# Building C times B with fp32 matmuls against a diagonal of the step, and splitting the last table steps by unit, in a long-convolution and attention kernel

## The chip, the cores and the metric

The kernel runs on one core of one Trainium2 chip. The metric is the device time of one execution in microseconds (us). Five engines run their own queues of instructions and wait for each other by semaphores: PE (TensorE, matmuls), DVE (VectorE), ACT (ScalarE), POOL (GpSimd) and SP, which here only issues DMAs.

## The reference, cut to what matters

The program adds four factors to a 2048 x 512 input: a state-space convolution (A), a windowed attention (B), A again and B again, each on a layer norm of what stands so far. The two A factors have the same parameters, so their convolution kernel `K` is made once, in the first factor.

```python
dt = jnp.exp(log_dt)[:, None]                  # 512 x 1
A = A_re + 1j * A_im; Bc = B_re + 1j * B_im; Cc = C_re + 1j * C_im
logdA = dt * A; dB = dt * Bc
P = jnp.exp(logdA[:, :, None] * l[None, None, :])     # l = 0..2047
K = jnp.einsum("dn,dnl,dn->dl", Cc, P, dB).real
...                                            # y = FFT convolution of u with K, over 2 L points
x = x + _A_ref(_layernorm(x), ...)
x = x + _B_ref(_layernorm(x), wqkv, wo)
x = x + _A_ref(_layernorm(x), ...)
x = x + _B_ref(_layernorm(x), wqkv, wo)
```

## The kernel before

The powers of `exp(dt A)` are not computed one by one. `prepare` makes the first power `LAM` and squares it nine times (`lads`), `Multipliers` keeps the powers as bf16 multipliers (`MYA`, `MYB`, `MXA`, `MSA` and so on), and `Tables` builds from them, for each of eight units of 64 channels, a Y table, an X table and a B table (`Ytab`, `Xtab`, `Btab`). `contract` multiplies the tables on PE into kernel samples (`psk`), ACT or DVE copies them out (`kq`), `select` places them (`pk`, `KT`), and a two-stage FFT (`spectrum`: `ps_s`, `Z`, `zt`, `xp`) turns them into `sp_k`. The normed input goes the same way into `sp_u`. DVE multiplies the two (`pa`), PE goes back (`vp`, `ps_y`) and `X` is overwritten.

The seed of the tables is `cb`, the complex product of C, B and dt, turned so that the state index lies on the partitions. Before, DVE forms four products (`t1` to `t4`), one difference, one sum and two products with dt, into slots 2 and 3 of `quad`. PE transposes the four slots (`ptq`): slots 1 and 0 become `LAM`, slots 2 and 3 become `cb`.

In `table_ops` a step of the recurrence (`y0` to `y2`, `a`, `b`, `d`, `e` for Y; `x1` to `x4` for X) is a product pair (`T.times`) and, except for `x4`, a sum (`T.add`). `CHUNKS` groups the units: 0, 1, 6 and 7 alone, 2 with 3 and 4 with 5. For a pair of units all steps but `x3` are one instruction over both, and every unit of the pair waits for all of it.

The order of the work is not made by a scheduler at build time. Each layer has a `Plan`: operations are numbered as they are declared, some in several ways (`pl.either`, `moved`: the same copy by ACT or by DVE), and a line of numbers in `ORDERS` says which are issued and in which order. The engines then take their parts of it strictly in that order. `psA`, `psk` are PSUM pools of 3 and 2 buffers.

Other names that are used below: `xT`, the input turned by DMA transposes for the layer-norm sums (`gram`); `wqk`, `wv`, the attention's weights, from which a mean is taken out in the first factor, for each third either by PE and two ACT copies (`ps_wc`, 20 matmuls) or by PE, ACT and a DVE sum (`ps_wm`, 4 matmuls; `wm`); `identf`, an fp32 identity; `ps_down`, a small plain fp32 matmul in each attention factor, one per factor, so two in the program.

Of the kernel before, what the change touches and what calls it, by code (L numbers as in the profile page):

```python
# [11 lines left out]
ACT = mybir.ActivationFunctionType  # L12
ALU = mybir.AluOpType
AX = mybir.AxisListType
F32 = mybir.dt.float32
# [13 lines left out]
NM = 128  # L29
# [202 lines left out]
def load_params(nc, pp, prm):  # L232
# [14 lines left out]

GATES = (13,)
ORDERS = [
# [265 lines left out]
def table_ops(pl, nc, T, u, n, seeds, free, fixed, casts):  # L515
    e = T.elements

    def step(what, *after):
        out = []
        for v, m in ((u, 1), (u + 1, 1)) if n == 2 and what == "x3" else ((u, n),):  # L520
            us, key = e(m, what) / 1920 + 0.069, ("sc", v, what)
            a = pl.op("V", 2 * us + (0.06 if what in ("y1", "y2", "x1", "x2") else 0), lambda v=v, m=m: T.times(v, m, what), *after, casts[T.POWER[what]], take=[] if what == "x4" else key)
            if what != "x4":
                a = pl.op("V", us, lambda v=v, m=m: T.add(v, m, what), a, drop=key)
            out.append(a)
        return out
    y = moved(pl, nc, ("seed", u), 0.15 + 0.1 * n, 0.08 + 0.066 * n, lambda copy: T.seed(copy, u, n), seeds, free)
    x = moved(pl, nc, ("second", u), 0.15 + 0.1 * n, 0.08 + 0.066 * n, lambda copy: T.second(copy, u, n), casts[3], free)
    for what in ("y0", "y1", "y2", "a", "b", "d", "e"):
        y = step(what, y)  # L530
    x = step("x1", x, fixed)
    for what in ("x2", "x3", "x4"):
        x = step(what, x)
    return [y, x]


def vt(n):
# [3 lines left out]
def prepare(nc, pl, lp, pp, psA, psK, raw, identf, block, ones, M, cb, T, ln, X, D2, marks):  # L541
# [5 lines left out]
    def vec(us, fn, *after, **needs):  # L547
        return pl.op("V", us, fn, *after, **needs)

    def tt(out, a, b, op):  # L550
        return lambda: nc.vector.tensor_tensor(out, a, b, op)

    def got(name):
        return pl.outer(("raw", name))
# [3 lines left out]
    tb, e, sh, sn, t1, t2, t3, t4 = [tmp(x) for x in ("tb", "e_mag", "sh", "sn", "t1", "t2", "t3", "t4")]  # L558
    lads = lp.tile([128, 9, D], F32, name="lads", tag="sp_u")
    rnd = lads[:, 8].rearrange("n (t m) -> n t m", t=4)  # L560
    quad = pp.tile([128, 4, 4, NM], F32, name="quad", tag="quad")
    LAM = pp.tile([128, 2, D], F32, name="LAM0", tag="LAM")
    wide = dtw[:].unsqueeze(2).to_broadcast([128, 4, NM])
    dt_bc = dtf[:].unsqueeze(2).to_broadcast([128, 4, NM])
# [14 lines left out]
    qs = [vec(0.61, lambda: nc.vector.scalar_tensor_tensor(quad[:, :, 0, :], sh[:], 1.0, e[:], ALU.subtract, ALU.mult), o, oe),  # L579
          vec(0.61, tt(quad[:, :, 1, :], e[:], sn[:], ALU.mult), on, oe)]  # L580

    def stepped(q, src, after):

        def by_rows():
            for t in range(4):
                nc.scalar.activation(quad[:, t, q, :], src[:, t, :], ACT.Copy, scale=dtf[:, t:t + 1])
        return pl.either(("step", q), lambda: pl.op("A", 1.3, by_rows, after, of),
                         lambda: vec(0.61, tt(quad[:, :, q, :], src[:], dt_bc, ALU.mult), after, of))
    raws = [got(x) for x in ("C_re", "B_re", "C_im", "B_im")]
    a = vec(0.61, tt(t1[:], raw["C_re"][:], raw["B_re"][:], ALU.mult), raws[:2])  # L590
    b = vec(0.61, tt(t2[:], raw["C_im"][:], raw["B_im"][:], ALU.mult), raws[2:])
    a = vec(0.61, tt(t1[:], t1[:], t2[:], ALU.subtract), a, b)
    qs.append(stepped(2, t1, a))
    a = vec(0.61, tt(t3[:], raw["C_re"][:], raw["B_im"][:], ALU.mult), raws[0], raws[3])
    b = vec(0.61, tt(t4[:], raw["C_im"][:], raw["B_re"][:], ALU.mult), raws[1:3])
    a = vec(0.61, tt(t3[:], t3[:], t4[:], ALU.add), a, b)
    qs.append(stepped(3, t3, a))
    turns, modes = [], {}
    for q in (1, 0, 2, 3):
        def mm(q=q):  # L600
            pt = box["pt", q] = psK.tile([128, 4, NM], F32, name="ptq", tag="psk")
            for t in range(4):
                nc.tensor.transpose(pt[:, t, :], quad[:, t, q, :], identf[:])

        def evac(copy, q=q):
            pt = box.pop(("pt", q))
            if q < 2:
                out, src = LAM[:, q, :].rearrange("n (p t) -> n p t", t=4), pt[:].rearrange("n t p -> n p t")
                if q:
                    copy(out, src)  # L610
                elif copy == nc.scalar.copy:
                    nc.scalar.activation(out, src, ACT.Copy, scale=-1.0)
                else:
                    nc.vector.tensor_scalar(out, src, -1.0, None, ALU.mult)
            else:
                copy(cb[:, :, q - 2, :], pt[:].rearrange("n t p -> n p t"))
        key = ("psk", "ptq", q)
        turns.append(pl.op("P", 1.15, mm, qs[q], got("identf"), take=key))
# [141 lines left out]
def kernel_and_first_conv(nc, tc, C, prm, x2d, const, kt_dram, eps, Wt):  # L760
    with ExitStack() as es:
# [311 lines left out]
        for u in range(8):  # L1073
            for u0, n in CHUNKS:
                if u0 == u:
                    o = table_ops(pl, nc, T, u0, n, marks["seeds"], [Cd[x - 2] for x in range(u0, u0 + n) if x > 1], marks["fixed"], marks["casts"])
                    for x in range(u0, u0 + n):
                        Td[x] = o
            contract(u)
            dc = u // 2  # L1080
            if dc == 3:
# [921 lines left out]
```

## Time and profile before

| | |
|---|---|
| median of 3 runs | 422.56 us (421.89 to 422.77) |
| the profiled execution | 420.84 us |
| span of its trace | 419.1 us |
| busy in the span: PE, DVE, ACT, POOL | 354.5, 390.4, 325.5, 29.0 us |
| mean granted PE clock | 0.97 |

The profiled execution lies 1.72 us under the median of the runs. The span is the trace's time from first to last instruction; the difference to the device time, 1.7 us, lies around it. In the timeline a row is start, length, engine, line of the kernel, operation, tiles, shape and count; the bracket gives the idle time before it and who ended it. Rows of the view by groups give busy time and the mean length of one in ns. On DVE and ACT the rows overlap by some 0.08 to 0.09 us, because the next instruction starts while the last one drains: a DVE row of 0.69 us takes 0.61 us of the queue.

### The profile page before, as it was taken

What the parts mean: (1) busy time and instruction counts of PE and PEld (TensorE: products, weight loads), DVE (VectorE), ACT (ScalarE), POOL (GpSimd) and SP (SyncE); (2) the same over time, 40 slices, a digit from 0 to 9 for tenths busy, and PEclk for the clock granted to TensorE, in tenths of its full rate; (3) what the DMA queues carried; (4) which work ended last, traced back from release to release, by engine and by line L of the source; (5) the groups of instructions that cost most, each with busy time, mean ns of one, the idle gap of its engine ahead of it and who ended that gap; (6) DMA issues with size and microseconds to landing.
All of it is one profiled execution on the core that took longest, in us unless ns stands there. A gap on an engine that the chain in (4) does not pass through costs nothing. (4 is left out here: it accounts for less than half of the span.)

```text
span 419.1 us, 13750 instructions
## 1 busy us (share of the span) xinstructions
PE 354.5 (85%) x5906; PEld 226.5 (54%) x5906; DVE 390.4 (93%) x643; ACT 325.5 (78%) x534; POOL 29.0 (7%) x99
## 2 busy tenths in 40 slices
PE   1367777887999989999975999899999999966995
PEld 1342555665787865446642444678864456632452
DVE  6999999799999897989999999999999999999994
ACT  6899999899899964678964589999966788762630
POOL 2000000000000200010100203020000010000321
PEclk9998899999999999999999899999999999995899
DMA  7998447987869977002334277799951000352396
GB/s 216 199 207 290 168 82 123 170 180 155 179 140 161 206 165 120 19 2 70 88 92 88 49 163 159 156 178 186 208 112 40 20 0 2 89 134 56 50 180 139
DMA packets 104914, 52.80 MB, mean 126 GB/s; under 512 B 84043, under 2 KB 96476, under 8 KB 104598
## 3 DMA queue, kind: packets, MB, share of 16 engines
q1 hardware_dynamic: 99014, 45.24, 49.9%
q0 software_dynamic: 3376, 5.37, 6.6%
q10 hardware_dynamic: 2464, 1.31, 1.1%
q8 instruction: 46, 0.75, 0.8%
q14 instruction: 14, 0.11, 0.1%
HBM read 19.30 MB, written 6.29 MB: 61 GB/s over the span
## 5 line engine op out<-in xcount | busy, mean ns | idle before, releaser
L1706 DVE TENSOR_TENSOR prod<-VX,L 128x512 bf16<-128x512 bf16 (+2 forms) x72 | 75.4, 1099 | 0.8 <-DMA VX<-VX 0.3
L1530 DVE TENSOR_TENSOR prod<-qT,kT 128x4096 bf16<-128x4096 bf16 (+1 forms) x40 | 72.3, 1855 | 0.5 <-ACT kT L1436 0.3
L877 ACT CAST Z<-ps_s 128x1024 bf16<-128x1024 f32 (+1 forms) x36 | 32.6, 944 | 1.5 <-PE ps_s L874 1.4
L1818 PE MATMUL ps_o<-wo_t,oT 128*32 128x512 bf16 x512 | 33.6, 395 | 0.0
L1485 PE MATMUL ps_v<-wv,U 128*128 128x256 bf16 x256 | 31.6, 272 | 1.7 <-ACT VX L1496 1.0
L1431 PE MATMUL ps_qk<-U,wqk 128*128 128x512 bf16 x128 | 30.3, 380 | 0.7 <-ACT qT L1436 0.7
L1496 ACT ACTIVATE VX<-ps_v,rs 128x256 bf16<-128x256 f32 x64 | 26.7, 471 | 3.8 <-PE ps_v L1485 3.0
L1485 PEld LDWEIGHTS <-U 128*128 128x128 bf16 x256 | 24.5, 97 | 9.6 <-issue 5.1
L1450 PE MATMUL ps_qk<-U,wqk 128*128 128x512 bf16 x128 | 28.8, 379 | 0.8 <-ACT X L1212 0.8
L1541 PE MATMUL Lp<-prod,sb_bones 128*32 128x512 bf16 x256 | 22.4, 412 | 5.7 <-DVE prod L1530 5.7
L1748 ACT CAST ot<-po 128x1024 bf16<-128x1024 f32 (+1 forms) x15 | 14.4, 985 | 14.3 <-PE po L1721 10.8
L1721 PE MATMUL po<-prod,sb_ident 32*32 32x512 bf16 x768 | 17.1, 428 | 7.7 <-DVE prod L1706 7.5
L969 DVE TENSOR_TENSOR pa<-sp_u,sp_k 128x2048 bf16<-128x2048 bf16 x16 | 19.2, 1221 | 4.0 <-ACT sp_k L905 2.8
L894 PE MATMUL xp<-zt,sb_C 128*128 128x512 bf16 x64 | 18.8, 379 | 4.7 <-ACT zt L914 2.2
L1818 PEld LDWEIGHTS <-oT 128*32 128x32 bf16 x512 | 13.3, 100 | 14.2 <-issue 3.8
L1431 PEld LDWEIGHTS <-wqk 128*128 128x128 bf16 x128 | 11.8, 98 | 17.0 <-issue 4.8
L1450 PEld LDWEIGHTS <-wqk 128*128 128x128 bf16 x128 | 12.4, 98 | 15.2 <-issue 1.1
L874 PE MATMUL ps_s<-KT,FK 128*128 128x128 bf16 (+1 forms) x360 | 18.9, 209 | 1.5 <-ACT KT L847 1.1
L1174 DVE TENSOR_TENSOR pa<-xc,Kt 128x2048 bf16<-128x2048 bf16 x16 | 18.9, 1217 | 0.6 <-PE vp L1186 0.3
L874 PEld LDWEIGHTS <-FK 128*128 128x128 bf16 x360 | 17.3, 98 | 3.3 <-issue 2.2
L905 ACT CAST sp_k<-xp 128x1024 bf16<-128x1024 f32 x16 | 16.2, 1029 | 2.3 <-PE xp L894 1.7
L983 PE MATMUL vp<-sb_IC,pa 128*128 128x128 bf16 x256 | 16.8, 219 | 1.4 <-ACT sp_k L905 0.7
(231 smaller groups left out, 862.4 us busy)
## 6 DMA issues: line engine op xcount, KB each, us to landing
kt_scratch<-sp_k SPq DMA_DIRECT2D x16, 256.0 KB, 3.1
Kt<-kt_scratch POOLq DMA_DIRECT2D x16, 256.0 KB, 5.9
sp_u<-sp_u SPq DMA_DIRECT2D x22, 128.0 KB, 3.2
X<-in_A_u_dram SPq DMA_DIRECT2D x8, 256.0 KB, 6.3
X<-in_A_u_dram SPq DMA_DIRECT2D x4, 512.0 KB, 5.2
Kt<-kt_scratch SPq DMA_DIRECT2D x8, 256.0 KB, 4.3
VX<-VX SPq DMA_DIRECT2D x4, 448.0 KB, 3.9
VX<-VX SPq DMA_DIRECT2D x4, 336.0 KB, 3.4
```

Source lines behind the costliest of these rows:

```text
L874: nc.tensor.matmul(ps[:, r, 0:n // 4, jj * 4:(jj + 1) * 4], w, x, start=(k == 0), stop=(k == len(todo) - 1))
L877: nc.scalar.copy(box["Z", kind, dc, b0][:, 0:n // 4, :, jq * 16:(jq + 1) * 16].rearrange("p g r k -> p r g k"), box.pop(("s1", kind, dc, j ...
L969: nc.vector.tensor_tensor(pr[:], box["U"][:, s:t + 1:t - s], k[:].unsqueeze(1).to_broadcast([128, 2, 1024]), ALU.mult)
L1174: nc.vector.tensor_tensor(pr[:], x[:].unsqueeze(1).to_broadcast([128, 2, 1024]), box.pop(("kt", dc, c))[:], ALU.mult)
L1431: nc.tensor.matmul(ps[:], wqk[:, ct, f0:f0 + 128], XT[:, ct // 2, 4 * s:4 * s + 4, ct % 2, :], start=(ct == 0), stop=(ct == 3))
L1450: nc.tensor.matmul(box[name][:, k * 512:k * 512 + 512], wqk[:, ct, f0:f0 + 128], XT[:, ct // 2, 4 * s:4 * s + 4, ct % 2, :], start=(ct == ...
L1485: nc.tensor.matmul(ps[:, jj].rearrange("p t h d -> p (t h d)"), XT[:, ct // 2, j + jj, ct % 2, :], wv[:, ct, fp * 256:(fp + 1) * 256], sta ...
L1496: nc.scalar.activation(out, ps, ACT.Identity, scale=r)
L1530: nc.vector.tensor_tensor(pr[:], windows(q, 0, 2), windows(kT[fp][:, a:a + n2, col(w):col(w) + 1024], -DIL * 128, 2), ALU.mult)
L1541: nc.tensor.matmul(Lp[r0:r0 + 32, w // 4, :], bones[:, w % 4 + k, :], pr[:, k, f2 - a, hb * 512:(hb + 1) * 512], start=(n == 1 and k == 0) ...
L1706: nc.vector.tensor_tensor(p2[:].rearrange("p w j t d h -> p w (j t) d h"), windows(v, -DIL * 256, taps), l.to_broadcast([128, taps, nj * 2 ...
L1818: nc.tensor.matmul(ps[r:r + 32], lhsT, rhs, start=(ft == -1 or ft == 0 and not res), stop=(ft == 3), skip_group_check=True)
```

## The change

It has four parts.

- The difference and the sum go into PE: `t2` is made with a minus sign (one instruction as before), and slots 2 and 3 of `quad` are no longer made. For each of four blocks PE multiplies `t1` and `t2` (then `t3` and `t4`) against `dg`, a diagonal matrix of dt, accumulating in PSUM. So 8 fp32 transposes become 16 plain fp32 matmuls, in a `psA` buffer and not in a `psk` one.
- `dg` (4 x 128 x 128, fp32) is made from `identf`; the chosen way is four ACT instructions.
- `x3` and `x4` of a pair of units are issued unit by unit, and each unit waits only for the Y chain and its own `x4`.
- `ORDERS` has a new line for the first factor (659 operations, 656 before), in which copies change between ACT and DVE, `wqk`'s query or key third moves from the DVE way to the PE way, and DMAs move. In the line of the second A factor one number, a small POOL copy, stands later; no engine's own order changes by it. From the end of the first factor on all engines have the same instructions as before.

```diff
-    def step(what, *after):
-        out = []
-        for v, m in ((u, 1), (u + 1, 1)) if n == 2 and what == "x3" else ((u, n),):
...
+    def step(v, n, what, *after):
...
-    x = step("x1", x, fixed)
-    for what in ("x2", "x3", "x4"):
-        x = step(what, x)
-    return [y, x]
+    for what in ("x1", "x2"):
+        x = step(u, n, what, x, fixed if what == "x1" else [])
+    return [[y, step(v, 1, "x4", step(v, 1, "x3", x))] for v in range(u, u + n)]
...
-    quad = pp.tile([128, 4, 4, NM], F32, name="quad", tag="quad")
+    quad = pp.tile([128, 4, 2, NM], F32, name="quad", tag="quad")
+    dg = pp.tile([128, 4, 128], F32, name="dg")
...
-    a = vec(0.61, tt(t1[:], t1[:], t2[:], ALU.subtract), a, b)
-    qs.append(stepped(2, t1, a))
+    qs.append([a, b, d])
...
-    a = vec(0.61, tt(t3[:], t3[:], t4[:], ALU.add), a, b)
-    qs.append(stepped(3, t3, a))
+    qs.append([a, b, d])
+    pairs = {2: (t1, t2), 3: (t3, t4)}
...
             for t in range(4):
-                nc.tensor.transpose(pt[:, t, :], quad[:, t, q, :], identf[:])
+                if q < 2:
+                    nc.tensor.transpose(pt[:, t, :], quad[:, t, q, :], identf[:])
+                for k, x in enumerate(pairs.get(q, ())):
+                    nc.tensor.matmul(pt[:, t, :], x[:, t, :], dg[:, t, :], start=(k == 0), stop=bool(k), skip_group_check=True)
...
-                        Td[x] = o
+                        Td[x] = o[x - u0]
```

In the ORDERS line of the first factor almost every number has moved; one line of it as it was and as it is:

```diff
-    "1 3 7 2 8 5 9 10 19 24 11 14 30 12 13 34 31 35 45 49 20 21 25 26 28 23 38 166 239 39 47 42 55 160 48 56 67 57 59 61 "
+    "1 3 7 2 243 162 8 9 158 5 10 26 23 12 242 13 11 14 25 24 32 34 156 28 16 29 43 45 36 40 168 48 172 46 57 65 160 66 "
```

Three places in the engines' queues follow. A number after a tile's name is a buffer's. The first is DVE near the start of the program, from the last products for `quad` to the first step of the squarings; before:

```order
L579 SCALAR_TENSOR_TENSOR quad<-sh,e_mag 128x4x128
L551 TENSOR_TENSOR t_141<-raw_C_im,raw_B_im 128x512
L551 TENSOR_TENSOR t_140<-t_140,t_141 128x512
L551 TENSOR_TENSOR t_143<-raw_C_im,raw_B_re 128x512
L551 TENSOR_TENSOR t_142<-t_142,t_143 128x512
L551 TENSOR_TENSOR quad<-t_142,dtf 128x4x128
L551 TENSOR_TENSOR quad<-t_140,dtf 128x4x128
L678 SCALAR_TENSOR_TENSOR lads<-LAM_146 128x512
```

And the same place now:

```order
L575 SCALAR_TENSOR_TENSOR quad<-sh,e_mag 128x4x128
L546 TENSOR_TENSOR quad<-e_mag,sn 128x4x128
L546 TENSOR_TENSOR t_142<-raw_C_re,raw_B_im 128x512
L585 SCALAR_TENSOR_TENSOR t_141<-raw_C_im,raw_B_im 128x512
L612 TENSOR_SCALAR LAM_147<-ptq 128x512
L676 SCALAR_TENSOR_TENSOR lads<-LAM_147 128x512
```

The sum, the difference and the two products with dt are gone from DVE's queue; one of the two copies of `LAM` out of PSUM, which was ACT's, stands there instead. The second place is ACT between the sines and the third squaring; before:

```order
L576 ACTIVATE sh<-lads 128x512
L577 ACTIVATE sn<-lads 128x512
L578 ACTIVATE sh<-sh 128x512
L610 COPY LAM_146<-ptq 128x512
L612 ACTIVATE LAM_146<-ptq 128x512
L670 ACTIVATE sq<-LAM_146 128x1024
L633 CAST MYA<-LAM_146 128x512
L616 CAST cb<-ptq 128x128x4
L670 ACTIVATE sq<-lads 128x1024
L633 CAST MYA<-lads 128x512
L616 CAST cb<-ptq 128x128x4
L670 ACTIVATE sq<-lads 128x1024
```

And now:

```order
L572 ACTIVATE sh<-lads 128x512
L574 ACTIVATE sh<-sh 128x512
L573 ACTIVATE sn<-lads 128x512
L580 ACTIVATE dg<-identf,dtf 128x128 x4
L608 COPY LAM_147<-ptq 128x512
L668 ACTIVATE sq<-LAM_147 128x1024
L637 ACTIVATE MYB<-LAM_147 128x128x4
L614 CAST cb<-ptq 128x128x4
L668 ACTIVATE sq<-lads 128x1024
L637 ACTIVATE MYB<-LAM_147 128x128x4
L614 CAST cb<-ptq 128x128x4
L668 ACTIVATE sq<-lads 128x1024
```

Four instructions for `dg` have come in, one `LAM` copy has gone, and the two copies of `cb` still stand each ahead of a squaring. The third place is DVE where units 2 and 3 get their last steps; before (MSA and MSB are multipliers, Tscr a scratch tile):

```order
L469 TENSOR_TENSOR Xtab_89<-Xtab_89,MSA_74 128x128x32
L476 TENSOR_TENSOR Btab_90<-Xtab_89,MSB_75 128x4096
L482 TENSOR_TENSOR Ytab_88<-Ytab_88,Tscr_1467 128x64x2x4
L969 TENSOR_TENSOR pa_1533<-sp_u_1339,sp_k_1531 128x2048
L969 TENSOR_TENSOR pa_1672<-sp_u_1339,sp_k_1529 128x2048
```

And now:

```order
L469 TENSOR_TENSOR Xtab_89<-Xtab_89,MSA_74 128x64x32
L476 TENSOR_TENSOR Btab_90<-Xtab_89,MSB_75 128x2048
L469 TENSOR_TENSOR Ytab_88<-Ytab_88,MSA_74 128x64x2x4
L476 TENSOR_TENSOR Tscr_1466<-Ytab_88,MSB_75 128x512
L482 TENSOR_TENSOR Ytab_88<-Ytab_88,Tscr_1466 128x64x2x4
L469 TENSOR_TENSOR Xtab_89<-Xtab_89,MSA_74 128x64x16
L476 TENSOR_TENSOR Tscr_1507<-Xtab_89,MSB_75 128x1024
L482 TENSOR_TENSOR Xtab_89<-Xtab_89,Tscr_1507 128x64x16
L469 TENSOR_TENSOR Xtab_89<-Xtab_89,MSA_74 128x64x32
L476 TENSOR_TENSOR Btab_90<-Xtab_89,MSB_75 128x2048
L967 TENSOR_TENSOR pa_1688<-sp_u_1356,sp_k_1681 128x2048
L967 TENSOR_TENSOR pa_1800<-sp_u_1356,sp_k_1697 128x2048
```

Unit 2 now has all its tables after the fifth of these rows, five instructions ahead of the first product, and unit 3 just ahead of it. Besides these, the DMA of `wqk` is issued on SP ahead of all eight transposes of `xT` (before, behind them), and on PE the matmuls that take the mean out of a third of `wqk` stand right behind `gram`, ahead of those of `wv`.

More of the change, by code (lines that the diff above doesn't have):

```diff
@@ L516, in table_ops @@
     e = T.elements
-    def step(what, *after):
-        out = []
-        for v, m in ((u, 1), (u + 1, 1)) if n == 2 and what == "x3" else ((u, n),):
[L521 to L526, printed above, removed]
+    def step(v, n, what, *after):
+        us, key = e(n, what) / 1920 + 0.069, ("sc", v, what)
+        extra = 0.06 if what in ("y1", "y2", "x1", "x2") else 0
+        a = pl.op("V", 2 * us + extra, lambda: T.times(v, n, what), *after, casts[T.POWER[what]], take=[] if what == "x4" else key)
+        return a if what == "x4" else pl.op("V", us, lambda: T.add(v, n, what), a, drop=key)
     y = moved(pl, nc, ("seed", u), 0.15 + 0.1 * n, 0.08 + 0.066 * n, lambda copy: T.seed(copy, u, n), seeds, free)
@@ L529, in table_ops @@
     for what in ("y0", "y1", "y2", "a", "b", "d", "e"):
-        y = step(what, y)
-    x = step("x1", x, fixed)
-    for what in ("x2", "x3", "x4"):
-        x = step(what, x)
-    return [y, x]
+        y = step(u, n, what, y)
+    for what in ("x1", "x2"):
+        x = step(u, n, what, x, fixed if what == "x1" else [])
+    return [[y, step(v, 1, "x4", step(v, 1, "x3", x))] for v in range(u, u + n)]
 def vt(n):
@@ L580, in prepare, with steps @@
           vec(0.61, tt(quad[:, :, 1, :], e[:], sn[:], ALU.mult), on, oe)]
[L582 to L588, printed above, removed]
+    def steps():
+        for t in range(4):
+            nc.scalar.activation(dg[:, t, :], identf[:], ACT.Copy, scale=dtf[:, t:t + 1])
+    d = pl.either(("dg",), lambda: pl.op("A", 0.85, steps, of, got("identf")),
+                  lambda: vec(0.61, tt(dg[:], identf[:].unsqueeze(1).to_broadcast([128, 4, 128]), dt_bc, ALU.mult), of, got("identf")))
     raws = [got(x) for x in ("C_re", "B_re", "C_im", "B_im")]
     a = vec(0.61, tt(t1[:], raw["C_re"][:], raw["B_re"][:], ALU.mult), raws[:2])
-    b = vec(0.61, tt(t2[:], raw["C_im"][:], raw["B_im"][:], ALU.mult), raws[2:])
-    a = vec(0.61, tt(t1[:], t1[:], t2[:], ALU.subtract), a, b)
-    qs.append(stepped(2, t1, a))
+    b = vec(0.61, lambda: nc.vector.scalar_tensor_tensor(t2[:], raw["C_im"][:], -1.0, raw["B_im"][:], ALU.mult, ALU.mult), raws[2:])
+    qs.append([a, b, d])
     a = vec(0.61, tt(t3[:], raw["C_re"][:], raw["B_im"][:], ALU.mult), raws[0], raws[3])
     b = vec(0.61, tt(t4[:], raw["C_im"][:], raw["B_re"][:], ALU.mult), raws[1:3])
-    a = vec(0.61, tt(t3[:], t3[:], t4[:], ALU.add), a, b)
-    qs.append(stepped(3, t3, a))
+    qs.append([a, b, d])
+    pairs = {2: (t1, t2), 3: (t3, t4)}
     turns, modes = [], {}
@@ L600, in mm @@
         def mm(q=q):
-            pt = box["pt", q] = psK.tile([128, 4, NM], F32, name="ptq", tag="psk")
+            pool, tag = (psK, "psk") if q < 2 else (psA, "psA")
+            pt = box["pt", q] = pool.tile([128, 4, NM] if q < 2 else [128, 2, 512], F32, name="ptq", tag=tag)
+            pt = box["pt", q] = pt if q < 2 else pt[:, 0].rearrange("n (t m) -> n t m", t=4)
             for t in range(4):
-                nc.tensor.transpose(pt[:, t, :], quad[:, t, q, :], identf[:])
+                if q < 2:
+                    nc.tensor.transpose(pt[:, t, :], quad[:, t, q, :], identf[:])
+                for k, x in enumerate(pairs.get(q, ())):
+                    nc.tensor.matmul(pt[:, t, :], x[:, t, :], dg[:, t, :], start=(k == 0), stop=bool(k), skip_group_check=True)
         def evac(copy, q=q):
@@ L616, in evac @@
                 copy(cb[:, :, q - 2, :], pt[:].rearrange("n t p -> n p t"))
-        key = ("psk", "ptq", q)
-        turns.append(pl.op("P", 1.15, mm, qs[q], got("identf"), take=key))
+        key = ("psk" if q < 2 else "psA", "ptq", q)
+        turns.append(pl.op("P", 1.15 if q < 2 else 2.1, mm, qs[q], got("identf"), take=key))
         modes[q] = moved(pl, nc, ("mode", q), 0.5, 0.61, evac, turns[-1], drop=key)
```

46 rows, old and new, of the table ORDERS are left out of this document.

## The prediction

> **What bounds the kernel now.** I read the page's head first, then the busy time by stretch, then the timeline of the first factor, because after it all queues are the same as before: whatever the first factor ends earlier or later, the whole program does.
>
> ```profile
> span 419.1 us, 13750 instructions
> 0.00:12.40 12.40, 1.97 (x8) 1.57 (x8) 8.27 (x14) 8.66 (x15) 2.12 (x11) 1.00 0.79 226
> 12.40:77.57 65.17, 45.06 (x1040) 30.88 (x1040) 62.45 (x151) 62.34 (x91) 0.00 (x0) 0.95 0.72 172
> 77.57:157.50 79.93, 71.75 (x1826) 58.30 (x1825) 75.09 (x151) 71.01 (x96) 2.10 (x4) 1.00 0.83 171
> ```
>
> The columns behind the length are PE, PE's weight loads, DVE, ACT, POOL, granted PE clock, DMA share and GB/s. From 12.40 to 77.57 us DVE and ACT are each busy 62 of 65 us, so a microsecond of work taken from both is nearly a microsecond of time, and a microsecond taken from one only helps until the other holds it up. From 77.57 on DVE (94%), PE (90%) and ACT (89%) wait for each other by turns. The factor's end is ACT's:
>
> ```profile
> 157.51 2.57 ACT L1009 CAST X<-ps_y 128x512 bf16<-128x512 f32 x4 [0.69 <-PE ps_y L1005]
> 158.13 0.69 DVE L200 BATCH_NORM_STATS2 ln_st_a<-X 128x6 f32<-128x512 bf16 x1 [1.04 <-ACT X L1009]
> ```
>
> ACT writes the last quarter of X, and DVE sits waiting for it. I therefore make the sum on ACT's queue and use DVE's as the counter-check.
>
> **The start.** This is the timeline around the squarings, all engines:
>
> ```profile
> 7.96 1.97 PE L603 MATMUL ptq<-identf,quad 128*128 128x128 f32 x8 [7.96 <-DVE quad L551]
> 9.11 0.58 ACT L610 COPY LAM<-ptq 128x512 f32<-128x512 f32 x1 [1.41 <-PE ptq L603]
> 9.96 0.60 ACT L612 ACTIVATE LAM<-ptq 128x512 f32<-128x512 f32 x1 [0.27 <-PE ptq L603]
> 10.47 0.69 DVE L551 TENSOR_TENSOR t<-t,t 128x512 f32<-128x512 f32 x1
> 10.59 1.06 ACT L670 ACTIVATE sq<-LAM 128x1024 f32<-128x1024 f32 x1
> 11.19 1.29 DVE L551 TENSOR_TENSOR quad<-t,dtf 128x512 f32<-128x512 f32 x2
> 12.40 0.69 DVE L678 SCALAR_TENSOR_TENSOR lads<-LAM 128x512 f32<-128x512 f32 x1
> 12.63 1.94 PE L603 MATMUL ptq<-identf,quad 128*128 128x128 f32 x8 [2.71 <-DVE quad L551]
> 13.76 0.58 ACT L616 CAST cb<-ptq 128x512 bf16<-128x512 f32 x1 [1.60 <-PE ptq L603]
> 16.18 1.06 ACT L670 ACTIVATE sq<-lads 128x1024 f32<-128x1024 f32 x1
> 17.28 0.69 DVE L682 TENSOR_TENSOR lads<-sq 128x512 f32<-128x512 f32 x1
> ```
>
> LAM is ready at 10.56 us, but DVE takes its first squaring step only at 12.40, because four instructions for C times B stand ahead of it. The change takes those four out: 4 x 0.61 = 2.4 us of DVE. It puts one LAM copy there (0.61). DVE's step can then start at about 10.75, 1.65 us earlier. ACT's first squaring stays at about 10.65: it waits for LAM either way, and the four `dg` instructions fit into the 1.41 us in which ACT idles before LAM. They have the shape of `e_mag`'s, 1.28 us for four.
>
> What the change adds stands on PE and is paid by whoever waits for `cb`. The trace of before has fp32 transposes, and two plain fp32 matmuls per program (`ps_down`):
>
> ```profile
> L603 PE MATMUL ptq<-identf,quad 128*128 128x128 f32 x16 | 3.9, 426 | 10.7 <-DVE quad L551 10.7
> L603 PEld LDWEIGHTS ptq<-identf,quad 128*128 128x128 f32 x16 | 3.1, 224 | 11.0 <-DVE quad L551 8.0 <-ACT MYA L633 3.1
> L1412 PE MATMUL ps_down<-rs,sb_down 128*128 128x14 f32 x4 | 0.7, 246 | 0.0
> L568 ACT ACTIVATE e_mag<-raw_A_re,dtf 128x128 f32<-128x128 bf16 x4 | 1.3, 389 | 0.0
> ```
>
> Sixteen transposes leave sixteen records, but two `ps_down` matmuls leave four: a plain fp32 matmul runs as two load-and-multiply pairs. Eight transposes take 1.97 us, 0.246 each, which is about the 0.224 of a weight load. So I price a plain matmul at 2 x 0.246 = 0.49 and a group of eight at 3.9 us. The bounds are 1.97 us (no dearer than transposes) and 10.4 us (16 x (0.224 + 0.426), no overlap at all); the row of x8 in 1.97 us shows overlap, so the doubled pace is nearest.
>
> PE is free for the first group at 9.95 us, when `t1`, `t2` and `dg` are there too. The group ends at about 14.05. ACT comes to this `cb` copy at 10.65 + 0.97 + 0.53 = 12.15 us and waits 1.9 us, where before it waited 1.60. The second group ends between 16.0 (transposes' pace) and 17.8 (doubled pace), and I take 16.9. ACT comes there at 14.05 + 0.5 + 0.97 + 0.53 = 16.05, waits 0.85, copies 0.5 and begins its third squaring at 17.4, against 16.18: **+1.2 us**. Bounds: 14.6 (−1.6) and 18.4 (+2.2).
>
> DVE is hit harder. Its difference of the third squares, at 17.28 before, has to wait until 17.4 + 1.0 = 18.4, and ahead of it stand 2 us less of DVE's work than before (2.4 out, 0.61 in, a few small rows moved): relative to its own work DVE is about 3.0 us late from there on, unit 0's and unit 1's tables included. Two covers hold because of it: the `gram` sums, and the mean of `wqk`.
>
> ```profile
> 27.74 0.43 SPq L1068 DMA_DIRECT2D wqk<-in_B_wqkv_dram  x1
> 30.24 0.30 PE L716 MATMUL gram<-xT 128*32 128x32 bf16 x16
> 33.00 1.91 PE L1057 MATMUL ps_wc<-wv,mones 128*128 128x512 bf16 x4
> 37.76 1.02 PE L1024 MATMUL ps_wm<-wqk,mones 128*128 128x512 bf16 x4 [2.84 <-DMA wqk<-in_B_wqkv_dram]
> 40.00:42.00 2.00, 2.00 (x6) 0.69 (x5) 2.00 (x7) 2.00 (x4) 0.00 (x0) 0.50 1.02 311
> 42.00:44.00 2.00, 0.82 (x4) 0.26 (x3) 2.00 (x6) 2.00 (x4) 0.00 (x0) 0.96 0.97 362
> ```
>
> `wqk`'s 1 MB now goes ahead of the `xT` transposes. At the 311 to 362 GB/s of the last two rows that is about 3 us of transfer, so `gram` ends near 33.5 and not 30.5. DVE needs it at about 34, so this costs nothing as long as DVE is late by the fp32 groups; if these were cheap, it would cost up to 2.4. PE then has 20 + 20 + 4 wide matmuls from about 34 on: 0.43 each at half clock (1.91 us for four), 0.21 at full (1.02 for four less the last one's tail), so between 9 and 19 us, and DVE brings unit 0's last table at about 48.5. In the middle of that it costs nothing; at its upper end up to 4 us.
>
> [...]
>
> **ACT's work.** Counted by form, ACT loses two norms of X, two `Ytab` copies, a LAM copy, two net multiplier copies, one copy each of `wm`, `kq` and `KT`; it gains `dg`, two `wqk` evacuations, half a VT and one `Xtab` copy.
>
> ```profile
> L731 ACT ACTIVATE X<-X,ln_nb_a,ln_rstd_a 128x512 bf16<-128x512 bf16 x13 | 9.8, 813 | 0.0
> L1060 ACT CAST wv<-ps_wc 128x1024 bf16<-128x1024 f32 x2 | 2.1, 1032 | 0.0
> L423 ACT COPY Ytab<-cb 128x256 bf16<-128x256 bf16 x2 | 0.9, 438 | 0.0
> L639 ACT ACTIVATE MXB<-lads 128x512 bf16<-128x512 f32 x4 | 2.5, 622 | 0.0
> L829 ACT CAST kq<-psk 128x320 bf16<-128x320 f32 x16 | 7.2, 448 | 2.1 <-PE psk L485 2.1
> ```
>
> With 0.09 us of overlap off each: −1.45 −0.70 −0.51 −1.02 −0.47 −0.36 −0.35 against +1.2 +1.88 +0.53 +0.37, together −0.9 us for the factor. Before the third squaring ACT has 0.7 us more (`dg` less the LAM copy), so from there on it has **−1.6 us**.
>
> **The split by unit.** The pair's last steps, what waits for them, and the price of a half:
>
> ```profile
> 70.17 2.28 DVE L469 TENSOR_TENSOR Xtab<-Xtab,MSA 128x4096 bf16<-128x4096 bf16 x1
> 72.37 2.28 DVE L476 TENSOR_TENSOR Btab<-Xtab,MSB 128x4096 bf16<-128x4096 bf16 x1
> 74.57 0.42 DVE L482 TENSOR_TENSOR Ytab<-Ytab,Tscr 128x512 bf16<-128x512 bf16 x1
> 75.61 1.93 ACT L905 CAST sp_k<-xp 128x1024 bf16<-128x1024 f32 x2 [0.68 <-PE xp L894]
> 77.57 2.36 DVE L969 TENSOR_TENSOR pa<-sp_u,sp_k 128x2048 bf16<-128x2048 bf16 x2 [2.58 <-ACT sp_k L905]
> 78.39 0.43 ACT L829 CAST kq<-psk 128x320 bf16<-128x320 f32 x1 [0.52 <-PE psk L485]
> 80.42 0.42 ACT L829 CAST kq<-psk 128x320 bf16<-128x320 f32 x1 [0.68 <-PE psk L485]
> L476 DVE TENSOR_TENSOR Btab<-Xtab,MSB 128x2048 bf16<-128x2048 bf16 x4 | 4.9, 1217 | 0.0
> ```
>
> Two halves cost 2 x 1.135 (1.217 less 0.08) against 2.20 start to start, 0.07 more; four such pairs, 0.28 us of DVE. In exchange unit 2 is complete 5.6 us earlier in DVE's own work, counted row by row with these lengths (both units' tables stood at 75.0). Even with DVE 3.0 late, PE can contract unit 2 about 2.5 us earlier than at 75. ACT's three waits here (0.68, 0.52, 0.68) are for PE's work of this stretch; I take **−0.8** of their 1.9 us, between 0 and −1.9. DVE's wait of 2.58 goes too: it would be ready at about 76 where it was at 75, and finds `sp_k` a little after.
>
> **The sum.** +1.2 −1.6 −0.8 = −1.2 us. From the profiled execution's 420.84 that gives 419.6; the same difference from the median of 422.56 gives **421.4 us**, and the forecast is for the median. DVE as counter-check: its first product comes 1.2 us earlier, at 76.4, but its work between first and last product grows by 1.6 us (more copies and later table steps stand there). If its 7.8 us of waits after 77.57 do not shrink, it ends 0.4 us late; they are waits on ACT and PE, so I expect them to.
>
> **Rivals.** (1) The fp32 matmuls are no dearer than the transposes: the third squaring starts at 14.6 instead of 17.4, 2.8 us better; the later `xT` takes 1.0 of that back. −3.0 us, 419.5. For it: the transposes are fp32 as well; against: the doubled records of `ps_down`. (2) The other side: DVE becomes the end. Both groups run at the doubled pace to 17.8 or beyond, so DVE loses another 0.9 to 1.3 us, and its 1.6 us more after the first product are not covered. +0.4 + 1.2 = +1.6 us, 424.2. It decides when the second group ends after about 17.5 us and DVE's waits after the first product stay near 7.8 us. For it: DVE is the busiest engine of both stretches; against: its last wait is for ACT. (3) The change does not reach the end: PE's hand-offs late in the factor, with new partners in a new order, swallow it. 422.5. For it: 90% of PE in the last stretch.
>
> **Chances.** The forecast 0.46, rival 1 0.12, rival 2 0.24, rival 3 0.18. The forecast's own range is 420.4 to 422.4, from the bounds of the second group and of ACT's waits. The full range, 419.4 to 424.2, takes in rival 1 and rival 2 at their middles and leaves 2 in 10 out. 0.2% is 0.85 us, about what a measurement of this kernel can tell from no change. Faster by more: rival 1 and four fifths of the forecast's case, 0.48; within: 0.26; slower: rival 2 and a little of rival 3, 0.26.
>
> **What would show it.** Right: the first `lads` step on DVE near 10.8 us; 32 records for 16 fp32 matmuls, eight of them in about 3.9 us; ACT's third squaring near 17.4; the wait before the first product under 1 us; ACT's last copy of X at about 156.3 and DVE waiting for it. Wrong: a third squaring under 15.5 (rival 1); a first product after 77.6, or DVE not waiting for ACT at the end (rival 2); a first product near 76.4 with the last X copy still at 157.5 (rival 3). The forecast falls too if PE's 44 wide matmuls reach past unit 0's tables, or if `gram` holds DVE after 34 us.

## The result, and the profile after

The changed kernel is slower: 427.5 us median (426.35 to 428.01, four runs) against 422.23 (420.88 to 422.77, four runs), a ratio of 1.0126 with a 95% interval of 1.0093 to 1.0159. Its profiled execution took 427.8 us. The forecast was 421.4. Medians and ratios in this document leave out two executions in a slower state of the chip, 449.52 us (a_pad224) and 1146 us (old_order).

These are the head of its page and rows of its timeline (start, length, engine, line, operation, tiles, shape; in brackets the idle time before and what ended it; lines from the table code on stand 2 lower than in before): the start, the hand-over to the first products, and the end of the factor.

```profile
span 426.0 us, 13790 instructions
10.27 5.15 PE L601 MATMUL ptq<-dg,t 128*128 128x128 f32 x32
11.13 0.69 DVE L676 SCALAR_TENSOR_TENSOR lads<-LAM 128x512 f32<-128x512 f32 x1 [0.27 <-ACT LAM L608]
16.09 1.07 ACT L668 ACTIVATE sq<-lads 128x1024 f32<-128x1024 f32 x1
77.87 1.22 DVE L967 TENSOR_TENSOR pa<-sp_u,sp_k 128x2048 bf16<-128x2048 bf16 x1
82.09 1.23 DVE L967 TENSOR_TENSOR pa<-sp_u,sp_k 128x2048 bf16<-128x2048 bf16 x1 [3.00 <-ACT sp_k L903]
163.72 2.57 ACT L1007 CAST X<-ps_y 128x512 bf16<-128x512 f32 x4 [0.69 <-PE ps_y L1003]
165.00 0.69 DVE L200 BATCH_NORM_STATS2 ln_st_a<-X 128x6 f32<-128x512 bf16 x1 [2.23 <-ACT X L1007]
```

The start did no harm: the third squaring begins at 16.09 us, against 16.18 in before. The first product begins at 77.87, against 77.57. Then the second product waits 3.00 us more, and the last copy of X begins at 163.72, 6.21 us later than before's 157.51. So the time was lost inside the first factor, nearly all of it behind 77 us. Three stretches show on whom. First before, then after (columns as in the prediction: length, PE, weight loads, DVE, ACT, POOL, granted clock, DMA share, GB/s):

```profile
50.00:60.00 10.00, 7.47 (x262) 6.35 (x262) 9.96 (x26) 10.00 (x16) 0.00 (x0) 1.00 0.22 50
80.00:90.00 10.00, 8.00 (x252) 5.99 (x249) 9.71 (x25) 9.25 (x15) 0.00 (x0) 1.00 0.89 155
140.00:150.00 10.00, 9.35 (x163) 7.66 (x161) 9.29 (x13) 8.25 (x12) 2.10 (x4) 1.00 0.91 195
```
```profile
50.00:60.00 10.00, 8.74 (x324) 7.81 (x322) 8.34 (x22) 7.72 (x12) 0.00 (x0) 0.84 0.37 44
80.00:90.00 10.00, 9.00 (x224) 7.52 (x225) 6.77 (x19) 6.20 (x9) 0.00 (x0) 0.66 0.80 142
140.00:150.00 10.00, 8.51 (x289) 7.16 (x288) 6.70 (x11) 6.78 (x12) 2.22 (x4) 1.00 0.81 192
```

In each of the three DVE and ACT, the busiest engines of before, now stand idle for 1.7 to 3.8 us each: they wait for PE. And PE's own timeline has, in or shortly before each, a stop for which it waits for nothing that the profile shows ("issue"). These are all of 0.5 us and more in after's first factor except one in the `gram` sums (1.82 us at 30.4, which nobody waited for), and then the largest of before:

```profile
57.76 0.39 PE L838 MATMUL pk<-kq,sb_ident 128*32 128x64 bf16 x19 [0.68 <-issue]
80.40 0.60 PE L892 MATMUL xp<-zt,sb_C 128*128 128x512 bf16 x2 [1.96 <-issue]
145.82 0.23 PE L981 MATMUL vp<-sb_IC,pa 128*128 128x128 bf16 x1 [1.14 <-issue]
```
```profile
79.88 0.50 PE L485 MATMUL psk<-Ytab,Btab 128*32 128x40 bf16 x26 [0.73 <-issue]
```

In the view of PE's waits between 12 and 165 us the rows that end in "issue" sum to 5.9 us in after and 1.6 us in before. What they are shows when PE's records (weight loads, matmuls and PE's 17 semaphore and drain instructions, in order of start) are counted. The stop of 0.73 us in before and the one of 1.96 us in after both fall ahead of record 2241, though different instructions stand there. The others of after fall at 705, 1473, 2497 and 5313. All are 193 more than a multiple of 256. So are all 60 stops of 0.25 us and more that end in "issue" in the twelve traces of this case that lack no PE records (the other four lack 25 to 30). The page's list of DMA queues has one that carries instructions, in packets of 16 KB:

```profile
q8 instruction: 46, 0.75, 0.8%
```

46 packets of 256 instructions are 11,776, about PE's 11,861 records. These are the times of its packets in the traces, beside PE's passing of every 256th record (us; "stood" is PE's idle time at the end of the block):

```
kernel   block entered  packet starts  lands   PE goes on  stood
after        27.43          29.69      30.65     32.18      1.82
after        54.06          55.15      56.32     57.76      0.68
after        75.55          77.80      78.94     80.40      1.96
after        80.40          81.49      82.63     84.13      0.27
after       141.54         143.34     144.44    145.81      1.13
before       76.22          77.38      78.26     79.88      0.73
before      106.47         107.50     108.52    109.94      0.37
before      109.94         111.12     112.60    113.94      0.55
```

Each row tells the same: 1.0 to 2.3 us after PE enters a block, the packet of the next one starts. It has landed 2.0 to 3.4 us after the entry, and PE goes on 1.3 to 1.6 us after that. In each of these rows PE had finished its 256 instructions by then, and it stood still for 0.27 to 1.96 us. In the twelve traces PE never entered a block sooner than 1.2 us after its packet had landed (546 fetches). A dense group of 64 short `psk` matmuls (128 instructions) takes 1.1 us (75.51 to 76.63 in before), so 256 of that kind last some 2.2 us, less than the fetch. The next three stretches are after's own between entering the block, the packet's start, its landing and PE's next instruction; in the last one PE does nothing:

```profile
75.55:77.80 2.25, 2.25 (x148) 1.75 (x136) 2.23 (x2) 2.25 (x5) 0.00 (x0) 1.00 0.97 222
77.80:78.94 1.14, 0.64 (x12) 0.11 (x2) 1.14 (x2) 1.14 (x3) 0.00 (x0) 1.00 1.95 146
78.94:80.40 1.46, 0.00 (x0) 0.00 (x1) 0.15 (x1) 0.14 (x1) 0.00 (x0) 1.00 0.46 97
```

The 46 packets of 16 KB and the spacing of the stops give the same unit, 256 instructions. Each stop ended 1.2 to 1.8 us after the very next packet had landed.

### The profile page after: what moved, and what is told of

Read it like the earlier page. It is cut to its first block, busy times and chain, and to the rows that moved or that the text cites. A ratio compares the mean times of both kernels' runs of the same rounds, so it can differ in the third digit from the quotient of the medians.

```text
span 426.0 us, 13790 instructions
## 1 busy us (share of the span) xinstructions
PE 361.0 (85%) x5922; PEld 235.0 (55%) x5922; DVE 389.8 (92%) x651; ACT 325.8 (76%) x532; POOL 29.1 (7%) x99
## 5 line engine op out<-in xcount | busy, mean ns | idle before, releaser
L1816 PE MATMUL ps_o<-wo_t,oT 128*32 128x512 bf16 x512 | 32.3, 382 | 0.4 <-DMA oT<-ot 0.2
L1746 ACT CAST ot<-po 128x1024 bf16<-128x1024 f32 (+1 forms) x15 | 14.4, 985 | 14.1 <-PE po L1719 10.5
L981 PE MATMUL vp<-sb_IC,pa 128*128 128x128 bf16 x256 | 17.8, 225 | 2.2 <-issue 1.1
```

Source lines behind the costliest of these rows:

```text
L1816: nc.tensor.matmul(ps[r:r + 32], lhsT, rhs, start=(ft == -1 or ft == 0 and not res), stop=(ft == 3), skip_group_check=True)
```

## The experiments

Theory A: the work is as good as before's, but the new order and the records that the change adds put PE's block ends into its dense groups. Theory B: the new order is slower by its waits between engines, and the stops are an accident beside them. Theory C: the fp32 matmuls or the halved steps cost the time. A shift of all block ends tells A from the others. It needs no change to the work: instructions ahead of everything on PE, while PE waits for its first operands (until 7.96 us in before, 8.50 in after).

```diff
+        pad = psK.tile([128, 1], F32, name="pad", tag="psk")
+        for _ in range(N):
+            nc.tensor.matmul(pad[0:1, 0:1], ones[:, 0:1], ones[:, 0:1], start=True, stop=True, ...)
         pl = Plan(psk=2, kq=2, psA=3, ...)
```

Each such matmul is two instructions, a weight load and a matmul (the trace of before has 5906 of each). All results, with PE's issue waits (12 to 165 us) and the start of the last copy of X from the profiled execution, whose own time is beside them:

| kernel | median us | ratio to before, 95% | profiled us | issue waits | last X copy |
|---|---|---|---|---|---|
| before | 422.23 | | 420.84 | 1.6 | 157.51 |
| after | 427.5 | 1.0126 (1.0093–1.0159) | 427.8 | 5.9 | 163.72 |
| b_pad256 | 422.22 | 1.0001 (0.9989–1.0014) | 421.0 | 2.4 | 157.92 |
| b_pad32 | 424.36 | 1.0066 (1.0047–1.0084) | 423.89 | 5.9 | 160.61 |
| b_pad80 | 432.69 | 1.0231 (1.0175–1.0286) | 433.49 | 8.0 | 166.96 |
| a_pad256 | 426.99 | 1.0119 (1.0102–1.0136) | 427.17 | 5.8 | 162.38 |
| a_pad80 | 425.27 | 1.0083 (1.0055–1.0111) | 423.12 | 1.6 | 156.69 |
| a_pad176 | 421.84 | 1.0002 (0.998–1.0025) | 423.86 | 2.6 | 159.93 |
| a_pad208 | 424.08 | 1.0046 (1.0017–1.0075) | 424.45 | 2.6 | 160.09 |
| a_pad224 | 424.6 | 1.0073 (1.0047–1.0099) | 423.29 | 3.1 | 159.04 |
| a_80_160 | 422.51 | 1.0014 (0.9994–1.0035) | 425.76 | 3.2 | 162.04 |
| old_order | 421.71 | 0.9992 (0.9977–1.0007) | 422.37 | 3.7 | 158.61 |
| old_order_raw | 426.42 | 1.0112 (1.0058–1.0167) | 427.59 | 6.4 | 163.40 |
| dve_sums | 424.53 | 1.0087 (1.0056–1.0118) | 428.43 | 5.4 | 160.96 |
| x_late | 426.28 | 1.0105 (1.0087–1.0122) | 426.6 | 4.8 | 163.48 |
| x_late2 | 426.26 | 1.0121 (1.0074–1.0167) | 426.68 | 4.9 | 162.15 |

**The first four shifts.**

> The kernel after, with 128 one-column matmuls (256 instructions, since each has its weight load) put ahead of everything on PE, while PE waits for its first operands. In the trace of after, PE stands still for 1.82, 0.68, 1.96 and 1.13 us (at 30.4, 57.1, 78.4 and 144.7 us) at its records 705, 1473, 2241 and 5313, which are 193 more than 2, 5, 8 and 20 times 256, and each time a 16 KB instruction transfer has landed about 1.4 us before it goes on. Theory A: PE's instructions come in blocks of 256, the next block is fetched when PE enters the one before it, and PE stops where it finishes a block sooner than the fetch. 256 more instructions leave the block ends on the same instructions: 427.5 within 0.8, same four stalls. Theory B (the stalls are not tied to blocks, or are not what costs the time; the new order is slower by its waits between engines): 427.5 too. This run is the control of the next one.

> The same with 104 matmuls (208 instructions): every block end moves by 208 instructions, that is 48 later in the old grid. Counted on after's own trace with a block time of 3.5 us below which PE stops, the sum of the stalls in the first factor falls from 3.9 to 1.7 us, and the one of 1.96 us at 78.4 goes. Theory A: 423.5 (422 to 425.5), and fewer stretches of half clock between 50 and 90 us. Theory B: 427.5 within 0.8, as the control.

> The kernel before, with 40 such matmuls (80 instructions) ahead on PE. By the same count on before's trace its block ends stand well now (1.7 us of stalls) and would stand worst after a shift of 80 (7.8 us, of which the largest at 50, 53, 80 and 124 us). Theory A: 425 to 429, slower than before with no change to any step of its work. Theory B: 422.2 within 0.8.

> The kernel before with 128 such matmuls (256 instructions), block ends on the same instructions as in before. Theory A: 422.2 within 0.8. Theory B: 422.2 within 0.8. If this run is slower than before, the one-column matmuls cost something by themselves (by the clock or by the start).

Both controls stayed, 426.99 and 422.22, so the one-column matmuls cost nothing. a_pad208 came down to 424.08. b_pad80 rose to 432.69, 10.5 us over its control, with no step of its work changed, more than Theory A had forecast. Its rows: PE's waits put down to issue (us in total, times, longest), its first products and its last copy of X.

```profile
PE psk L485 <- issue: 4.6, 4, 1.9
PE pk L843 <- issue: 1.7, 2, 1.2
PE gram L716 <- issue: 1.2, 1, 1.2
PE ps_s L877 <- issue: 0.5, 1, 0.5
81.45 2.36 DVE L972 TENSOR_TENSOR pa<-sp_u,sp_k 128x2048 bf16<-128x2048 bf16 x2 [4.71 <-ACT sp_k L908]
166.96 2.57 ACT L1012 CAST X<-ps_y 128x512 bf16<-128x512 f32 x4 [0.69 <-PE ps_y L1008]
```

8.0 us of stops where before has 1.6, and the factor ends 9.45 us later. Theory B cannot give that.

a_pad256 settles a second question. After's granted clock falls to 0.84 and 0.66 in two of the stretches above; is that the cause? Here are 40 to 100 us, first of after, then of a_pad256:

```profile
40.00:100.00 60.00, 47.54 (x1112) 36.84 (x1109) 53.82 (x114) 51.88 (x70) 0.00 (x0) 0.89 0.60 128
```
```profile
40.00:100.00 60.00, 45.84 (x1150) 34.82 (x1148) 55.92 (x119) 54.43 (x73) 0.00 (x0) 1.00 0.62 140
```

a_pad256 had the full clock throughout this stretch, about the same sum of stops (5.8 us), and 427.17 us in this execution against after's 427.8. So the clock here was worth at most about 0.6 us. Between 12 and 40 us the view shows a lower clock for after than for before, too (0.70 against 0.98, though before's clock records begin only at 35.3 us); old_order, below, has 0.70 there and before's time. What is left as the cause is the stops.

**The same shift on both kernels, and a smaller one.**

> The kernel after with 40 one-column matmuls (80 instructions) ahead on PE, the shift at which the kernel before took 432.7 us. Counted on after's traces, this shift leaves its block ends about as bad as they are (sum of stalls 6.1 to 7.1 us against 6.8 to 7.5 without a shift). Theory A (blocks of 256): 427.5 (426 to 429), so that at this shift the change would read as 1.2% faster instead of 1.3% slower. Rival (80 such matmuls cost time by themselves, by the clock or the start): 435 or more, as much above after as before rose above 422.

> The kernel before with 16 one-column matmuls (32 instructions, about the 31 records that the change adds). Counted on before's traces a shift of 32 raises the sum of stalls by 2.6 us, where a shift of 80 raised it by 6.4 and the time by 10.7. Theory A: 425 (423.5 to 427). Rival (a shift matters only at the worst place): 422.

At a shift of 80 the changed kernel took 425.27 and the kernel before 432.69: there the change reads as 1.4% faster (1.0083 over 1.0231 is 0.986, with both intervals 0.979 to 0.992), without a shift as 1.3% slower. The rival, that the matmuls cost time by themselves, is out. a_pad80 came out better than counted, and its profiled execution was its fastest (423.12). Two rows of it matter for the prediction, its first products and its last copy of X; then comes a stop far behind the factor, in code that the change doesn't touch:

```profile
76.44 2.35 DVE L970 TENSOR_TENSOR pa<-sp_u,sp_k 128x2048 bf16<-128x2048 bf16 x2
156.69 2.57 ACT L1010 CAST X<-ps_y 128x512 bf16<-128x512 f32 x4 [0.69 <-PE ps_y L1006]
244.78 1.04 PE L1722 MATMUL po<-prod,sb_ident 32*32 32x512 bf16 x51
247.91 0.43 PE L1722 MATMUL po<-prod,sb_ident 32*32 32x512 bf16 x13 [2.09 <-issue]
```

b_pad32, a shift by about as many records as the change adds (31), took 424.36, 2.9 us over before in the same runs (421.48), where 425 was forecast.

**The code without the order, and the order without the fp32 sums.** old_order gives the changed code the order of before. Its list is before's with the operations renumbered, the four sums and steps of DVE left out, `dg` put ahead of ACT's first LAM copy, and each pair's last product written as two:

```diff
-    x3(u)  x3(u+1)  x4(u and u+1)
+    x3(u)  x3(u+1)  x4(u)  x4(u+1)
```

dve_sums does the reverse: after's order, with the sums on DVE, for `t1` as below and for `t3` alike.

```diff
-                    nc.tensor.matmul(pt[:, t, :], x[:, t, :], dg[:, t, :], ...)
+                    nc.tensor.transpose(pt[:, t, :], pairs[q][0][:, t, :], identf[:])
+        nc.vector.tensor_tensor(t1[:], t1[:], t2[:], ALU.subtract)
+        nc.vector.tensor_tensor(t1[:], t1[:], dt_bc, ALU.mult)
```

> The change's code (dg, fp32 sums, last table steps unit by unit) in the order of before: every instruction of the first factor stands where it stood in before, the pair's last product is now two halves one behind the other, dg goes ahead of ACT's LAM copies, and DVE's four instructions between the raw products and the first lads step are gone. 104 one-column matmuls ahead on PE, with the 48 more records of the fp32 matmuls, bring the block ends to the instructions where before has them. Theory A (after is slow because its order meets the block ends badly): 421 to 422.3; near 421.0 if DVE's 1.2 us at the start reach the end, 422.0 if a wait swallows them. Theory C (the fp32 matmuls or the halved steps themselves cost the time): 424 or more.

> The kernel after with its order, but the sums and the step of C times B on DVE as in before (three DVE instructions more for each of the two products, dg and the plain fp32 matmuls left out, eight fp32 transposes in their place), and 128 one-column matmuls ahead on PE, so that the block ends stand as in a_pad208 (424.1 us). If the fp32 sums help the start as DVE's queue says (its first lads step 1.3 us earlier): 425.3. If the waits behind the start swallow it: 424.1 within 0.8. If the fp32 matmuls cost time: below 423.5.

> old_order without the 104 one-column matmuls: the change's code in the order of before, its block ends now 48 instructions off those of before, since each of the 16 plain fp32 matmuls is four records where two transposes were four. Counted on before's traces a shift of 48 raises the sum of stalls by 3.7 us (8.1 against 4.2 in the mean over fetch times of 2.9 to 4.9 us). Theory A: 425 to 429. Rival (only the order decides, the 104 matmuls do nothing): 421.7 as old_order.

old_order took 421.71, before's time, with its block ends where before has them. Without the 104 matmuls, 48 instructions off, the same kernel took 426.42: the fp32 matmuls cost 4.7 us there, none of it by their work. (A plain fp32 matmul leaves four records, a transpose two: 64 records stand for 16.) So Theory C falls, and the order is not needed for the loss either. Rows of old_order and then of dve_sums show what the sums on PE did for the start, DVE's first squaring step and ACT's second and third squarings:

```profile
10.59 0.69 DVE L677 SCALAR_TENSOR_TENSOR lads<-LAM 128x512 f32<-128x512 f32 x1 [0.88 <-ACT LAM L611]
13.77 1.06 ACT L669 ACTIVATE sq<-lads 128x1024 f32<-128x1024 f32 x1
15.71 1.07 ACT L669 ACTIVATE sq<-lads 128x1024 f32<-128x1024 f32 x1
```
```profile
13.51 0.69 DVE L688 SCALAR_TENSOR_TENSOR lads<-LAM 128x512 f32<-128x512 f32 x1
15.45 1.06 ACT L680 ACTIVATE sq<-lads 128x1024 f32<-128x1024 f32 x1
17.39 1.06 ACT L680 ACTIVATE sq<-lads 128x1024 f32<-128x1024 f32 x1
```

In before the first step stood at 12.40 and the third squaring at 16.18. The sums on PE bring 1.8 us of DVE's start and 0.5 us of ACT's in old_order, and neither reaches the end (421.71 against 421.72 in the same runs). Taking them away in after's order costs 1.3 us at the third squaring (17.39 against 16.09), and 424.53 against a_pad208's 424.08 at the end. The ratios, 1.0087 and 1.0046, have intervals that overlap, so these runs can't tell whether that is a difference.

**What delays a fetch.** In x_late and x_late2 one entry of SP's list moves.

```diff
-    X<-in_A_u (512 KB)
     zt<-Z, kt store, zt<-Z, kt store, zt<-Z, kt store
+    X<-in_A_u (512 KB)
```

> The kernel after with one step moved on SP's queue: the first reload of X from memory (512 KB, issued at 74.0 us) goes behind the third store of kt (issued at 86.0 us); what needs it starts at 107 us. In after the fetch of the block that PE waits for at 78.4 us starts 2.25 us after PE has entered the block before (75.55 to 77.80), while DMA is busy; elsewhere it starts after 0.3 to 1.3 us. Theory A with a fetch that queues behind other DMA work: it starts within 1.3 us, the stall of 1.96 us falls to 0.5 to 1.2 us, and the time to 426.3 (425.3 to 427). Rival (the start of a fetch doesn't depend on what the DMA engines carry): the stall stays near 2 us and the time at 427.5.

> In x_late the reload that moved was the one issued at 63.6 us; the one at 74.0 us stayed (72.99 there), the fetch still began 2.50 us after the block before was entered, and PE stood still 2.43 us at the same block end. Here the reload at 74.0 us itself goes behind the third store of kt (86.0 us). Theory A with fetches that queue behind other DMA work: the fetch starts 0.8 to 1.5 us after the block before is entered instead of 2.25, the stall of 1.96 us falls to 0.3 to 1.3 us, the second product comes 1 to 2 us sooner than at 82.1, and the time is 426 (424.5 to 427). Rival (the fetch's delay there has another cause): stall near 2 us, 427.5.

x_late moved the wrong one of the four reloads (the one issued at 63.6 us), so its expectation wasn't put to the test. The reload of 74 us stayed (at 72.99), and so did the stop:

```profile
79.62 1.04 PE L894 MATMUL xp<-zt,sb_C 128*128 128x512 bf16 x2 [2.43 <-issue]
```

x_late2 moved the right one. The packet started 0.84 us after the block before was entered, not 2.25 (2.27 at the same block in a_pad256 and 2.50 in x_late, both with the reload in its place), the stop fell from 1.96 to 0.86 us, and the second product came at 80.57, not 82.09. (The row puts its 0.86 us down to ACT's `kq`, which ended at 78.66; the packet had landed at 77.40, which is 1.49 us before, as in the other stops.) But the next block end took most of it back, 1.18 us where after had 0.27:

```profile
78.89 0.61 PE L894 MATMUL xp<-zt,sb_C 128*128 128x512 bf16 x2 [0.86 <-ACT kq L829]
80.57 1.23 DVE L969 TENSOR_TENSOR pa<-sp_u,sp_k 128x2048 bf16<-128x2048 bf16 x1 [0.92 <-ACT sp_k L905]
82.89 0.20 PE L487 MATMUL psk<-Ytab,Btab 128*32 128x40 bf16 x2 [1.18 <-issue]
```

The time, 426.26, is where it was forecast, 1.2 us under after. But x_late came as low without its stop being gone, and against before in the same runs x_late2 is at 1.0121, after at 1.0126. So the later fetch beside the reload is shown, at this one block; its worth at the end is not. Nor does the expectation's "elsewhere 0.3 to 1.3 us" hold: after's other packets started between 1.9 us before and 4.2 us after PE entered the block before.

**What the new order is worth when the block ends fall well.**

> a_pad80 (40 one-column matmuls ahead on PE) with 40 more behind the last ps_y matmul of the first factor, where PE waits 0.67 us for ACT. In a_pad80 the first factor ended 0.8 us sooner than in before (last copy of X at 156.69 against 157.51), but 2.85 us were lost at 246 to 258 us, where PE stood 2.09 us at a block end inside 64 short po matmuls that the change doesn't touch. 80 more instructions move that block end out of them. Theory A: no such stall, the time 2 to 3 us under a_pad80's 425.3: 422.7 (421 to 424), and in its best executions below before's 421.5. Theory D (the new order is slower by its own waits, whatever the block ends): 424 or more.

> The kernel after with 88 one-column matmuls (176 instructions) ahead on PE: by the count on the traces no block end inside the short po matmuls later (0.0 us of stalls there), and 3.9 to 4.9 us in the first factor, where the unshifted kernel counts 6.8 to 7.5 and before 3.8 to 4.4. Theory A: between before and a_pad208: 423 (421.5 to 424.5). Theory D: 424 or more.

> The same with 112 matmuls (224 instructions): 0.0 us counted later, 3.1 to 4.7 us in the first factor. Theory A: 423 (421.5 to 424.5). Theory D: 424 or more.

a_pad176 took 421.84, with before at 421.63 in the same runs: a ratio of 1.0002 (0.998 to 1.0025). a_80_160 took 422.51, 2.8 us under a_pad80, about what a_pad80's later stop had cost; its trace has no such stop. So the whole loss of 5.3 us goes away without a change to the work or the order, at the best of the five shifts tried on after, and the change itself is worth nothing that can be measured. a_pad224 was a miss, 424.6 where 423 (421.5 to 424.5) was forecast: with b_pad80 and a_pad80 it shows that the count of stops from other traces is good to some 2 to 4 us only. At some shifts single executions also spread by 4 to 6 us (a_pad176: 419.17 to 424.47), where before's spread by 3 (420.07 to 422.88 in the same runs). No version beat the kernel before by more than can be measured; old_order and a_pad176 equal it.

## Why the prediction was wrong

- **The step that failed is the sum.** It held three terms for ACT's queue and named PE only as a partner of waits. It had no term for PE's supply of instructions, and that was worth +5.2 us (after at 1.0126 of before, a_pad176, with the same work and order, at 1.0002). The profile of before had the signs: the stop of 0.73 us with no releaser in the hand-over to the first products, and the 46 packets on an instruction queue. Rival 3 (PE's hand-offs swallow the gain) came nearest, but it went no further than "no change" and put the cause on order and partners.
- **Third squaring at 17.4, +1.2 us: mis-sized.** The record count was right (32 for 16 matmuls), the pace was nearly right for half of them only. In after the records start 0.213 us apart up to 13.24 us, just like the transposes ahead of them, and 0.111 us apart from there. The trace's first clock record, of the full clock, begins at 13.23. The 0.246 was too high because the eight transposes' 1.97 us has the length of the last one, 0.42 us, in it. The first group ended at 13.64 us, where 14.05 was predicted. The second ran nearly all at the fast pace and ended at 15.42, before the 16.9 that was taken. The squaring began at 16.09, so the term was −0.1.
- **DVE's first step at 10.75:** 11.13 in after, where the transposes started at 8.50 instead of 7.96. Right in old_order, 10.59.
- **The covers held.** `gram` ended at 32.4 and DVE did not wait for it. PE's 44 wide matmuls stood from 32.78 to 45.0, inside the 9 to 19 us, and unit 0's last table came at 47.6, after them.
- **ACT's −1.6 us and the −0.8 of the split** stay open. One execution is in line with them, a_pad80's profiled one, with before's 1.6 us of issue waits: its first product began at 76.44, where 76.4 was predicted, without a wait, and the last copy of X at 156.69, where 156.3 was predicted and before had 157.51. That is in part luck: it was the fastest of that kernel's four. The same instructions up to the end of the factor, in a_80_160's profiled execution (the slowest of its twelve), met 3.2 us of issue waits, and brought the first product at 78.23 and the last copy at 162.04. In after the first product came at 77.87 and the next one waited 3.00 us behind a stop of 1.96.
- **The −1.2 us is not shown as a gain of the kernel.** At the two best shifts the time equals before's. Since the stops change from run to run, it stays open whether some tenths of a per cent of the predicted gain are in there.
- **"Wrong if the first product comes after 77.6"** was given as the sign of rival 2 (DVE becomes the end). The sign came, but DVE was not the end: it waited for ACT at the end (2.23 us) and stood idle more than before.

## What to carry to other kernels

Before a small reordering is judged on a kernel whose PE runs long groups of short matmuls, look for PE stops put down to "issue" and count whether they sit 256 records apart; if so, run both versions at two or three shifts (some one-column matmuls ahead of the program, and 256 instructions as the control). A difference of one per cent at a single alignment says little: the same change read +1.3% and −1.4% here. Before's order depends on its block ends, too: 32 more instructions ahead of it cost 2.9 us here.

## What the runs showed of the hardware

- PE's instructions come in blocks of 256 (16 KB) over a DMA queue of their own: 46 packets for 11,861 records in after. The packet of the next block starts about when PE enters the one before; over 558 fetches of the twelve complete traces the time between them ran from 3.2 us before to 4.8 us after, half of it between 0.2 and 1.5 us after. In the first factor, of the packets that started after PE's passing, the delay was 0.89 us in the mean where the other DMA queues had kept the engines under 5% busy in the microsecond before (42 packets), and 1.50 us where they had been fully busy (106). A packet took 0.9 to 1.9 us (median 1.1), and in the stops PE went on 1.2 to 1.8 us after it landed. From these means a block of 256 instructions that PE runs in less than some 3.4 to 4.1 us makes it stand still (an estimate: 0.89 or 1.50, and 1.1 and 1.45).
- A stop can cost more than itself: b_pad80's stops in the first factor were 6.4 us longer than before's, and its factor ended 9.45 us later. Nor does every stop count: after's 1.82 us in the `gram` sums cost nothing that the trace shows.
- A plain fp32 matmul of 128x128 left two matmul records, a transpose one. Per record they had the same pace, 0.213 us from start to start, and it became 0.111 us where the trace's clock record begins with the full clock: at 13.2 us in after, 13.0 in old_order, 13.8 in a_pad256.
